# Attention and PReLU layer on one core: units 8 to 17 in five two-unit visits instead of nine groups, with a new order of chunks 1 to 3

## The chip, the core and the metric

The kernel runs on one core of a Trainium2 chip. The metric is the device time of one execution in microseconds. Five engines work side by side and wait for each other through semaphores: TensorE (PE in the profile, its weight loads PEld), VectorE (DVE), ScalarE (ACT), GpSimd (POOL) and SyncE (SP), which here only issues transfers. Each engine works through its own instructions in the order of the program.

## The reference

Linear attention with a decay per head, in blocks of positions with a running state, and behind it a two-layer network with a PReLU. Inputs are q, k and v of (4 batches, 8 heads, 768 positions, 64), a decay per head, and the weights.

```python
intra = np.einsum('bhic,bhjc->bhij', qb, kb) * Dmask[None]
intra = np.einsum('bhij,bhjd->bhid', intra, vb)
inter = np.einsum('bhid,bhde->bhie', qb * lam_pow[None], kv_state)
out[:, :, sl] = intra + inter
kv_state = lam_block[None, :, None, None] * kv_state + np.einsum('bhsd,bhse->bhde', kb * rev_pow[None], vb)
...
h = x @ w_in                                             # x: (3072, 512), w_in: (512, 2048)
g = np.maximum(h, 0.0) + alpha * np.minimum(h, 0.0)
return g @ w_out                                         # w_out: (2048, 512)
```

## The kernel before

**Units and chunks.** A unit is one batch, four heads and 256 positions; there are 24. Four units (two batches, both halves of the heads) make a chunk of 512 rows of x; there are six chunks, 0 to 5, and units 4c to 4c+3 belong to chunk c. Chunks 0 and 1 hold the first 256 positions of the batches, 2 and 3 the next, 4 and 5 the last, so unit n+8 needs the state that unit n leaves. The kernel's blocks are 128 positions long, two to a unit.

**What a unit takes.** `load(c, bi, x)` brings k, q or v of two units by a transfer from SP. `cast` makes fp16 copies on ScalarE, VectorE or GpSimd (its last argument A, V or G); `key_decayed` makes k times its decay (kdec, L284). `transposes` turns q and k over (qkT): with "D" by a DMA from SP (L302), else on TensorE with a copy. `decayed` makes q times its decay, qdT (L350), and from chunk 2 on also qdX (L362, two on GpSimd), the same rows for the other half of the partitions. The state R of a unit is kept in fp16; RX is a copy of it with the partition halves exchanged (L491, L625, GpSimd).

**Groups on TensorE.** The attention matmuls use quarters of the array (64x64). `cluster(old, new)` (L372) takes one earlier unit and one new one: the old unit's output from the state (L398), the new one's scores (L415), the old one's output from masked scores (L427), and the new one's state product (L442); then VectorE masks the scores (sm, L453) and updates R (L478), and the output is copied to xT. `visit(olds, news, engs)` (L541) takes up to two of each with one set of switches: per old unit 8 + 16 output matmuls (L509, L521), per new one 16 scores (L593) and 32 state matmuls for two (L573). The first new unit's scores lie in banks s0 and s1, the second's in tk and op, and the first old unit's outputs in two banks h. The masks (L603) follow each scores group on VectorE; the state is updated later, by `settle(n)` (L615, L625). Before, units 16 to 23 go by visits, 8 to 15 by clusters.

**The network.** `up(c, f)` is four full matmuls of 128x512 (L746) into a bank, `m = relu(-h)` on ScalarE (L756) and, at once or later by `slope_product`, `g = (1 - alpha) m + h` on VectorE (L778). A bank is free again when its slope is done; h has two, the others (op, tk, s0, s1) one each. `down(c, t, part, 4)` is four matmuls over f = 4 part to 4 part + 3 (L793); four parts make one output tile, which ScalarE copies (L806) and SP stores, at once or by `store_held`.

**The order** is written out by hand: one list of calls, L833 to the end, is the program, and each engine takes its own instructions in the order of the list. Ups and downs of the chunk before lie between the attention groups. Tiles have a few buffers each (qkT, qdT and qdX three, fp16 casts and kdec four, masks two for each half, acc one), so a call also waits for the last reader of the buffer that it takes. An instruction that waits holds up everything behind it on its engine, on SP too.

Of the kernel before, what the change touches and what calls it, by code (L numbers as in the profile page):

```python
# [11 lines left out]
def kernel(  # L12
# [24 lines left out]
    B, H, S, D = q.shape  # L37
# [503 lines left out]
    def visit(olds, news, engs, banks=("tk", "op")):  # L541
# [191 lines left out]
    G = {}  # L733
# [232 lines left out]
    up(0, 5, None, "op", True)  # L966
    slope_product(0, 5, None)
    load(1, 1, "v", None)
    gate(1, "out")
    transposed(4, 1, "A", "tk")  # L970
    up(0, 13, None, "h")
    transposes(5, "A", False)
    decayed(5, "G")
    cast(7, "k16", "G")
    load_wout(2)
    cluster(None, 4)
    up(0, 15, None, "h")
    up(0, 9, None, "op", True)
    slope_product(0, 9, None)
    up(0, 12, None, "h", True)  # L980
    cast(6, "k16", "A")
    load_wout(3)
    slope_product(0, 12, None)
    gate(3, "in")
    key_decayed(6, "G")
    cluster(4, 5, "A")
    cast(6, "q16", "A")
    down(0, 0, 0, 4, "h")
    down(0, 2, 0, 4, "op")
    transposes(6, "A", False)  # L990
    load(2, 0, "k", None)
    cast(7, "q16", "G")
    cluster(5, None, "A")
    down(0, 3, 0, 4, "h")
    decayed(6, "G")
    transposes(7, "V", False)
    up(1, 6, 0, "s1")
    up(1, 5, 0, "s0")
    down(0, 1, 0, 4, "tk")
    down(0, 2, 1, 4, "op")  # L1000
    cast(6, "v16", "V")
    decayed(7, "G")
    cast(8, "k16", "G")
    key_decayed(7, "V")
    down(0, 3, 1, 4, "h")
    cluster(None, 6)
    cast(7, "v16", "A")
    load(2, 1, "q", None)
    cast(11, "q16", "G")
    down(0, 2, 2, 4, "op")  # L1010
    down(0, 0, 1, 4, "h")
    load(2, 0, "q", None)
    cast(9, "k16", "G")
    cast(8, "q16", "G")
    cluster(6, 7, "A")
    load(2, 1, "k", None)
    key_decayed(10, "G")
    down(0, 0, 2, 4, "h")
    query_decay(2, 0)
    down(0, 2, 3, 4, "op")  # L1020
    down(0, 1, 1, 4, "tk")
    down(0, 1, 2, 4, "tk")
    cluster(7, None, "A")
    key_decayed(8, "V")
    down(0, 1, 3, 4, "tk", True)
    load(2, 0, "v", None)
    cast(8, "v16", "G")
    key_decayed(9, "G")
    up(1, 6, 1, "op")
    transposes(8, "D", False)  # L1030
    load(3, 0, "k", None)
    down(0, 0, 3, 4, "h", True)
    down(0, 3, 2, 4, "h")
    store_held(0, 0)
    query_decay(1, 0)
    cast(10, "k16", "A")
    decayed(8, "G")
    cast(9, "q16", "A")
    up(1, 5, 1, "tk", True)
    transposes(9, "D", False)  # L1040
    cast(11, "k16", "G")
    slope_product(1, 5, 1)
    up(1, 7, None, "op", True)
    slope_product(1, 7, None)
    up(1, 13, None, "h")
    cast(10, "q16", "G")
    down(0, 3, 3, 4, "h")
    cluster(None, 8)
    store_held(0, 1)
    decayed(9, "G")  # L1050
    cast(9, "v16", "A")
    up(1, 10, None, "tk")
    up(1, 1, None, "h", True)
    slope_product(1, 1, None)
    up(1, 4, None, "op")
    up(1, 11, None, "h")
    load(2, 1, "v", None)
    transposes(10, "D", False)
    up(1, 9, None, "tk")
    cluster(8, 9, "A")  # L1060
    up(1, 0, None, "op", True)
    slope_product(1, 0, None)
    decayed(10, "G")
    up(1, 8, None, "h")
    up(1, 2, None, "h")
    cast(10, "v16", "A")
    cast(11, "v16", "G")
    up(1, 3, None, "tk")
    up(1, 15, None, "op", True)
    slope_product(1, 15, None)  # L1070
    up(1, 12, None, "h")
    transposes(11, "D", False)
    decayed(11, "G")
    key_decayed(12, "V")
    load(3, 0, "q", None)
    cast(13, "q16", "A")
    load(3, 1, "q", None)
    load(3, 0, "v", None)
    cluster(9, 10, "V")
    up(1, 14, None, "tk")  # L1080
    key_decayed(13, "V")
    down(1, 2, 0, 4, "h")
    cast(12, "v16", "A")
    down(1, 0, 0, 4, "h")
    down(1, 0, 1, 4, "h")
    down(1, 2, 1, 4, "h")
    down(1, 0, 2, 4, "h")
    down(1, 2, 2, 4, "h")
    cast(12, "k16", "V")
    load(3, 1, "k", None)  # L1090
    cast(14, "q16", "A")
    cast(14, "k16", "A")
    load(4, 0, "k", None)
    down(1, 1, 0, 4, "op")
    cast(12, "q16", "G")
    cast(13, "k16", "A")
# [230 lines left out]
```

## Time and profile before

| | us |
|---|---|
| median of three runs (211.29 to 212.5) | 212.08 |
| the profiled execution: its own time | 212.1 |
| its span, first to last instruction | 210.3 |
| TensorE busy | 203.0 |
| VectorE busy | 130.9 |
| ScalarE busy | 118.9 |
| GpSimd busy | 98.1 |

The granted TensorE clock is 0.999. The page gives an engine's busy time as a share of the span. The chain of waits follows the work that ended last back to its start; in its rows stand start, length and piece, and what it calls PE is time in which nothing but TensorE's own matmuls set the end. A view of an engine in order of time gives start, length, line, operation, output and input, and in brackets the idle time before it with what ended it. In views that group instructions stand mean or min/median/max in ns.

### The profile page before, as it was taken

The page shows a single profiled execution, that of the slowest core. Times are in us where ns is not written, and L with a number is a line of the kernel's source. Part 1 is how long each engine was busy: PE and PEld are TensorE (multiplying, and loading weights), DVE is VectorE, ACT ScalarE, POOL GpSimd, SP SyncE. Part 2 cuts the span into 40 slices and gives each one's busy share as a digit, 9 for nine tenths or more (in the row PEclk, how much of TensorE's full clock was granted, in tenths as well). Part 3 has the DMA queues.
Part 4 walks back from the last instruction along what each step waited for, and adds up shares of the span by engine and source line. Part 5 has one row for each costly group of instructions (what it writes and reads, how often), then busy time and mean ns, then how long its engine had stood idle before and what let it go on. Part 6 is the DMA issues. An engine that isn't in the chain of part 4 may idle for free.

```text
span 210.3 us, 5338 instructions
## 1 busy us (share of the span) xinstructions
PE 203.0 (97%) x2145; PEld 103.4 (49%) x2145; DVE 130.9 (62%) x254; ACT 118.9 (57%) x231; POOL 98.1 (47%) x155
## 2 busy tenths in 40 slices
PE   7896999999999999999999999999999999999994
PEld 7463445645545545455454544544544444444442
DVE  7894689575299959779968774654754444444000
ACT  4995679734777454567757546565533643444121
POOL 7286088415498846589806728529464000000000
PEclk9999999999999999999999999999999999999999
DMA  5999999999999999799539999123101101110212
GB/s 156 299 280 204 227 270 269 210 261 274 222 301 167 304 218 260 174 251 221 113 107 211 232 226 228 51 51 100 51 4 53 50 2 50 53 50 0 100 50 103
DMA packets 62335, 33.91 MB, mean 161 GB/s; under 512 B 18134, under 2 KB 59366, under 8 KB 62310
## 3 DMA queue, kind: packets, MB, share of 16 engines
q1 hardware_dynamic: 58038, 29.37, 55.9%
q0 software_dynamic: 4224, 4.19, 12.1%
q8 instruction: 17, 0.28, 0.6%
q14 instruction: 8, 0.07, 0.1%
q10 hardware_dynamic: 48, 0.01, 0.0%
HBM read 27.27 MB, written 6.29 MB: 160 GB/s over the span
## 4 chain that ended last, share of the span: by engine, by line
PE 90%; DMA 3%; ACT 2%; SPq 1%; issue 1%; DVE 1%; POOL 0%; ACTq 0%
PE h_ps L746 40%; PE o_ps L793 32%; PE o_ps L822 7%; DMA vraw<-in_v_dram 3%; SPq L93 1%; PE s L415 1%; PE acc L427 1%; PE unread L147 1%; PE tp L312 1%; PE s L593 1%; PE acc L398 1%; PE acc L442 1%; PE acc L675 1%; PE acc L521 1%; ACT xT L254 1%
## 5 line engine op out<-in xcount | busy, mean ns | idle before, releaser
L778 DVE SCALAR_TENSOR_TENSOR g<-m,oma,h_ps 128x512 f16<-128x512 f32 (+1 forms) x98 | 70.8, 735 | 46.1 <-ACT m L756 43.6
L746 PE MATMUL h_ps<-xT,w_in_sb 128*128 128x512 f16 (+1 forms) x392 | 92.4, 375 | 0.1
L756 ACT ACTIVATE m<-h_ps 128x512 f32<-128x512 f32 (+1 forms) x98 | 57.5, 587 | 44.2 <-PE h_ps L746 42.4
L793 PE MATMUL o_ps<-w_out_sb,g 128*128 128x512 f16 x320 | 78.3, 379 | 0.0
L746 PEld LDWEIGHTS <-w_in_sb 128*128 128x128 f16 x392 | 37.2, 98 | 42.4 <-issue 0.6
L793 PEld LDWEIGHTS <-g 128*128 128x128 f16 x320 | 30.7, 98 | 36.2 <-issue 0.2
L350 POOL TENSOR_TENSOR qdT<-qkT,qdecay 128x512 f16<-128x512 f16 (+1 forms) x22 | 22.1, 1007 | 15.4 <-ACT qkT L254 10.5
L806 ACT ACTIVATE o_sb<-o_ps 128x512 f32<-128x512 f32 (+2 forms) x25 | 14.5, 580 | 22.4 <-PE o_ps L793 11.4
L362 POOL TENSOR_TENSOR qdX<-qkT,qdecay 64x256 f16<-64x256 f16 x32 | 22.4, 701 | 2.3
L453 DVE TENSOR_TENSOR sm<-s,dmask 128x512 f16<-128x512 f32 x24 | 15.4, 683 | 4.5 <-PE s L415 4.5
L284 POOL TENSOR_TENSOR kdec<-kraw,kdecay 128x512 f16<-128x512 f32 x14 | 14.6, 1047 | 3.4 <-DMA kraw<-in_k_dram 3.1
L254 ACT ACTIVATE xT<-acc 128x512 f16<-128x512 f32 x18 | 10.7, 596 | 8.7 <-PE acc L442 4.0
L625 POOL COPY RX<-R 64x128 f16<-64x128 f16 x16 | 5.0, 310 | 21.4 <-DVE R L615 20.7
L822 PE MATMUL o_ps<-w_out_sb,g 128*128 128x512 f16 (+2 forms) x80 | 14.0, 336 | 0.0
L603 DVE TENSOR_TENSOR sm<-s,dmask 128x512 f16<-128x512 f32 x16 | 9.9, 684 | 5.0 <-PE s L593 5.0
L822 PEld LDWEIGHTS <-g 128*128 128x128 f16 x80 | 7.2, 98 | 6.9
L258 POOL CAST qk<-qraw 128x512 f16<-128x512 f32 x13 | 8.0, 618 | 2.3 <-DMA qraw<-in_q_dram 2.0
L478 DVE SCALAR_TENSOR_TENSOR R<-R,rdecay,acc 128x64 f16<-128x64 f16 x40 | 8.6, 273 | 0.4 <-ACT R L475 0.4
L254 ACT ACTIVATE v<-vraw 128x512 f16<-128x512 f32 x12 | 7.5, 624 | 2.5 <-POOL RX L491 2.5
L258 POOL CAST qk<-kraw 128x512 f16<-128x512 f32 x9 | 6.0, 662 | 6.1 <-DMA kraw<-in_k_dram 6.0
L491 POOL COPY RX<-R 64x128 f16<-64x128 f16 x16 | 6.0, 373 | 5.5 <-DVE R L478 4.8
L258 POOL CAST v<-vraw 128x512 f16<-128x512 f32 x10 | 6.2, 628 | 4.8 <-DMA vraw<-in_v_dram 4.5
(96 smaller groups left out, 165.8 us busy)
## 6 DMA issues: line engine op xcount, KB each, us to landing
out_dram<-o_sb SPq DMA_DIRECT2D x23, 256.0 KB, 3.0
qraw<-in_q_dram SPq DMA_DIRECT2D x10, 512.0 KB, 7.5
kraw<-in_k_dram SPq DMA_DIRECT2D x10, 512.0 KB, 8.1
vraw<-in_v_dram SPq DMA_DIRECT2D x10, 512.0 KB, 5.6
w_in_sb<-in_moe_w_in_dram POOLq DMA_DIRECT2D x4, 512.0 KB, 9.6
w_out_sb<-in_moe_w_out_dram POOLq DMA_DIRECT2D x4, 512.0 KB, 8.4
kraw<-in_k_dram SPq DMA_DIRECT2D x4, 256.0 KB, 4.2
qraw<-in_q_dram SPq DMA_DIRECT2D x4, 256.0 KB, 4.7
```

Of the source, the lines that this page charges most:

```text
L254: nc.scalar.activation(out, in_, AF.Copy)
L258: nc.gpsimd.tensor_copy(out=out, in_=in_)
L284: engine(eng).tensor_tensor(out=kdec, in0=kr, in1=kdecay[:, ds(4 * hh, 4), :].rearrange("p h e -> p e h").unsqueeze(3).to_broadcast([128, ...
L350: engine(eng).tensor_tensor(out=qdT[:, :, :, p], in0=t["qkT"][:, 0, :, :, p], in1=qdecay[:, hh, :, :, p], op=ALU.mult,)
L362: nc.gpsimd.tensor_tensor(out=qdX[block], in0=t["qkT"][other, 0, :, :, block], in1=qdecay[other, hh, :, :, block], op=ALU.mult,)
L453: nc.vector.tensor_tensor(out=sm, in0=s[hl], in1=mask_of(hl, hh), op=ALU.mult)
L746: nc.tensor.matmul(h_ps[:, 0:n] if bi is None else h_ps[:, 0:n].rearrange("p (e j) -> p e j", e=2), lhsT=w_in_sb[:, gi, ts(f, 128)], rhs=x ...
L756: nc.scalar.activation(m[:, 0:n], h_ps[:, 0:n], AF.Relu, scale=-1.0)
L778: nc.vector.scalar_tensor_tensor(out=g, in0=mv, scalar=oma[:, f : f + 1], in1=hv, op0=ALU.mult, op1=ALU.add)
L793: nc.tensor.matmul(o_ps, lhsT=lhs(c, f, t), rhs=w_out_sb[:, f, :], start=(f == 0), stop=(f == NF - 1),)
L806: nc.scalar.activation(o_sb[:, 0:n], o_ps[:, 0:n], AF.Copy)
L822: nc.tensor.matmul(o_ps[:, 0:n], lhsT=lhs(c, f, t), rhs=w_out_sb[:, f, ds(x, n)], start=(f == 0), stop=(f == NF - 1),)
```

## The change

The list of calls is rewritten from chunk 0's end to chunk 3, and `visit` now also takes two new units with no old one. The diff, cut to its core (the list is told below):

```diff
@@ visit
         if olds:
             outs_to_xt(olds[-1], view, engs[len(olds) - 1])
+        elif news:
+            wide_scores(news[0], ("s0", "s1"))
         for n in news[1:]:
             wide_scores(n, banks)
@@ the list of calls, five of its lines
-    cluster(None, 8)
-    cluster(8, 9, "A")
...
-    visit([15], [16, 17], "A")
+    visit([], [8, 9], "")
...
+    visit([14, 15], [16, 17], "AA")
```

- Nine groups, cluster(None, 8), (8, 9), (9, 10) and so on to (14, 15), and visit([15], [16, 17]), become five visits: ([], [8, 9]), ([8, 9], [10, 11]), ([10, 11], [12, 13]), ([12, 13], [14, 15]) and ([14, 15], [16, 17]). The states of units 8 to 17 are now updated by `settle`.
- up(0, 15) stands before the opening cluster of unit 4, not between it and cluster(4, 5). After cluster(None, 6) come three downs instead of two.
- Ups 10, 1, 4, 11, 9 and 0 of chunk 1 stand before the first visit, ups 8, 3, 2, 15, 14 and 12 and four downs between the first and the second, eight downs before the third, seven ups and four downs before the fourth, nine ups and four downs before the fifth.
- Many casts and key products change engine: the key product of unit 10 goes from GpSimd to VectorE, and stands behind the slope of up(1, 13).
- The transposes of 8 and 9, of 12 and 13, and of 15 and 14 follow each other on SP. Some stores are held longer.

Three places of the order follow. First, VectorE around the opening cluster of unit 4, before; the g rows are slopes of chunk 0, here 14, 5 and 13, then masks and state of unit 4, then slopes 15, 9 and 12, then masks and state of unit 5:

```order
L778 SCALAR_TENSOR_TENSOR g_777<-m,oma,h_ps 128x512
L778 SCALAR_TENSOR_TENSOR g_792<-m,oma,h_ps 128x512
L778 SCALAR_TENSOR_TENSOR g_809<-m,oma,h_ps 128x512
L453 TENSOR_TENSOR sm_862<-s_828,dmask 128x512
L453 TENSOR_TENSOR sm_864<-s_829,dmask 128x512
L478 SCALAR_TENSOR_TENSOR R_0_2_116<-R_0_1_115,rdecay,acc 128x64 x2
L778 SCALAR_TENSOR_TENSOR g_878<-m,oma,h_ps 128x512
L778 SCALAR_TENSOR_TENSOR g_887<-m,oma,h_ps 128x512
L778 SCALAR_TENSOR_TENSOR g_899<-m,oma,h_ps 128x512
L453 TENSOR_TENSOR sm_957<-s_907,dmask 128x512
L453 TENSOR_TENSOR sm_959<-s_908,dmask 128x512
L478 SCALAR_TENSOR_TENSOR R_1_2_121<-R_1_1_120,rdecay,acc 128x64 x2
```

The same place after; the slopes are 14, 15, 5 and 13, then unit 4, slope 9, and unit 5:

```order
L780 SCALAR_TENSOR_TENSOR g_777<-m,oma,h_ps 128x512
L780 SCALAR_TENSOR_TENSOR g_799<-m,oma,h_ps 128x512
L780 SCALAR_TENSOR_TENSOR g_801<-m,oma,h_ps 128x512
L780 SCALAR_TENSOR_TENSOR g_827<-m,oma,h_ps 128x512
L453 TENSOR_TENSOR sm_882<-s_848,dmask 128x512
L453 TENSOR_TENSOR sm_884<-s_849,dmask 128x512
L478 SCALAR_TENSOR_TENSOR R_0_2_116<-R_0_1_115,rdecay,acc 128x64 x2
L780 SCALAR_TENSOR_TENSOR g_905<-m,oma,h_ps 128x512
L453 TENSOR_TENSOR sm_962<-s_912,dmask 128x512
L453 TENSOR_TENSOR sm_964<-s_913,dmask 128x512
L478 SCALAR_TENSOR_TENSOR R_1_2_121<-R_1_1_120,rdecay,acc 128x64 x2
```

Slope 15 has moved ahead of slope 5 and of the masks and the state of unit 4, and slope 12 behind unit 5; between the two groups one slope is left of three.

Second, VectorE where unit 8 is opened, before; the slopes are 7 and 13 of chunk 1, then masks and state of unit 8, slopes 10, 1, 4, 11 and 9, and the mask of unit 9:

```order
L778 SCALAR_TENSOR_TENSOR g_1307<-m,oma,h_ps 128x512
L778 SCALAR_TENSOR_TENSOR g_1316<-m,oma,h_ps 128x512
L453 TENSOR_TENSOR sm_1361<-s_1327,dmask 128x512
L453 TENSOR_TENSOR sm_1363<-s_1328,dmask 128x512
L478 SCALAR_TENSOR_TENSOR R_0_3_97<-R_0_2_96,rdecay,acc 128x64 x2
L478 SCALAR_TENSOR_TENSOR R_0_4_98<-R_0_3_97,rdecay,acc 128x64 x2
L778 SCALAR_TENSOR_TENSOR g_1386<-m,oma,h_ps 128x512
L778 SCALAR_TENSOR_TENSOR g_1395<-m,oma,h_ps 128x512
L778 SCALAR_TENSOR_TENSOR g_1404<-m,oma,h_ps 128x512
L778 SCALAR_TENSOR_TENSOR g_1413<-m,oma,h_ps 128x512
L778 SCALAR_TENSOR_TENSOR g_1425<-m,oma,h_ps 128x512
L453 TENSOR_TENSOR sm_1486<-s_1436,dmask 128x512
```

After; the slopes are 11 and 9, then the masks of units 8 and 9 by the visit, slope 0, the state of unit 8, and slopes 8, 3 and 2:

```order
L780 SCALAR_TENSOR_TENSOR g_1372<-m,oma,h_ps 128x512
L780 SCALAR_TENSOR_TENSOR g_1381<-m,oma,h_ps 128x512
L605 TENSOR_TENSOR sm_1441<-s,dmask 128x512
L605 TENSOR_TENSOR sm_1443<-s,dmask 128x512
L605 TENSOR_TENSOR sm_1463<-s,dmask 128x512
L605 TENSOR_TENSOR sm_1465<-s,dmask 128x512
L780 SCALAR_TENSOR_TENSOR g_1467<-m,oma,h_ps 128x512
L617 SCALAR_TENSOR_TENSOR R_0_3_97<-R_0_2_96,rdecay,acc 128x64 x2
L617 SCALAR_TENSOR_TENSOR R_0_4_98<-R_0_3_97,rdecay,acc 128x64 x2
L780 SCALAR_TENSOR_TENSOR g_1482<-m,oma,h_ps 128x512
L780 SCALAR_TENSOR_TENSOR g_1494<-m,oma,h_ps 128x512
L780 SCALAR_TENSOR_TENSOR g_1503<-m,oma,h_ps 128x512
```

Four masks now stand together, with the slopes of 8, 3 and 2 behind them and the state of unit 8; the state of unit 9 comes later still.

Third, SP from the loads of chunk 2 on, before; the loads are k of units 8 and 9, q of both pairs, k of 10 and 11, and behind the store v of 8 and 9, and the transposes are those of 8, 9, 10 and 11:

```order
L93 DMA kraw<-in_k_dram 128x8x128
L93 DMA qraw<-in_q_dram 128x8x128 x2
L93 DMA kraw<-in_k_dram 128x8x128
L815 DMA out_dram<-o_sb 128x512
L93 DMA vraw<-in_v_dram 128x8x128
L302 DMA_TRANSPOSE qkT<-qk_1064 128x8x128
L93 DMA kraw<-in_k_dram 128x8x128
L815 DMA out_dram<-o_sb 128x512
L302 DMA_TRANSPOSE qkT<-qk_1133 128x8x128
L815 DMA out_dram<-o_sb 128x512 x2
L93 DMA vraw<-in_v_dram 128x8x128
L302 DMA_TRANSPOSE qkT<-qk_1281 128x8x128
```

After; the loads are q of both pairs, k of 8 and 9, and behind the store v of 8 and 9, k of 12 and 13, k of 10 and 11, the transposes are those of 8, 9 and 10, and the 1x1 transfer is a gate, which only waits for a part of the weights:

```order
L93 DMA qraw<-in_q_dram 128x8x128 x2
L119 DMA gates_153<-w_in_sb 1x1
L93 DMA kraw<-in_k_dram 128x8x128
L817 DMA out_dram<-o_sb 128x512
L93 DMA vraw<-in_v_dram 128x8x128
L93 DMA kraw<-in_k_dram 128x8x128 x2
L302 DMA_TRANSPOSE qkT<-qk_1209 128x8x128
L302 DMA_TRANSPOSE qkT<-qk_1231 128x8x128
L817 DMA out_dram<-o_sb 128x512 x2
L93 DMA vraw<-in_v_dram 128x8x128
L93 DMA kraw<-in_k_dram 128x8x128
L302 DMA_TRANSPOSE qkT<-qk_1318 128x8x128
```

The load of k of units 10 and 11 has moved from ahead of the first store to behind v of 8 and 9 and k of 12 and 13; the transposes of 8 and 9 stand behind it, side by side.

More of the change, by code (lines that the diff above doesn't have):

```diff
@@ L1005 @@
[L1005 to L1012, printed above, removed]
+    cluster(7, None, "A")
     cast(9, "k16", "G")
     cast(8, "q16", "G")
[L1015 to L1021, printed above, removed]
+    cast(11, "q16", "G")
+    key_decayed(9, "G")
@@ L1072 @@
+    load(3, 0, "q", None)
+    store_held(0, 0)
     transposes(11, "D", False)
[L1073 to L1076, printed above, removed]
     load(3, 1, "q", None)
     load(3, 0, "v", None)
[L1079 to L1088, printed above, removed]
```

332 lines of the change are left out of this document (177 added, 155 removed).

## The prediction

> **What bounds the kernel now.** I read the page's busy shares first, then its slices, then stretches of time engine by engine, then the chain of work that ended last. The page:
>
> ```profile
> PE 203.0 (97%) x2145; PEld 103.4 (49%) x2145; DVE 130.9 (62%) x254; ACT 118.9 (57%) x231; POOL 98.1 (47%) x155
> DMA  5999999999999999799539999123101101110212
> ```
>
> TensorE is busy for 203.0 of 210.3 us, and the DMA engines are at nine tenths or more in nearly all of the first half, where the change lies. Stretches show where TensorE still waits, and what is near it (after the colon: stretch, then busy time of PE, PEld, DVE, ACT, POOL).
>
> ```profile
> 30.00:40.00 10.00, 9.84 (x151) 5.51 (x148) 8.92 (x17) 8.84 (x20) 7.68 (x11) 1.00 1.19 245
> 40.00:120.00 80.00, 80.00 (x1028) 40.61 (x1021) 61.00 (x122) 48.65 (x93) 50.50 (x75) 1.00 0.97 220
> 60.00:70.00 10.00, 10.00 (x142) 4.99 (x143) 9.76 (x21) 7.43 (x13) 8.76 (x15) 1.00 1.05 233
> ```
>
> From 40 to 120 us TensorE has no gap; from 30 to 40 it lacks 0.16 us. So the only things that can move the time are matmul time itself and new gaps. And VectorE, at 9.76 of 10, has nothing to spare just where the first new visit comes. The chain gives TensorE's own cost of a cluster and a visit (start, length, piece):
>
> ```profile
> 57.60 0.86 PE o_ps L793 x4
> 58.47 0.35 PE s L415 x16
> 58.94 4.42 PE h_ps L746 x20
> 63.36 0.24 PE acc L398 x8
> ...
> 64.17 5.29 PE h_ps L746 x24
> ...
> 71.23 6.91 PE o_ps L793 x32
> ...
> 106.88 0.24 PE acc L509 x8
> ...
> 108.03 2.78 PE h_ps L746 x12
> ...
> 118.58 0.24 PE ot L509 x8
> ...
> 120.07 0.97 PE h_ps L746 x4
> ```
>
> Four full matmuls take 6.91 / 8 = 0.863 us. A cluster with an old and a new unit runs from 63.36 to 64.17, and the 24 matmuls behind it take 5.29 where 6 x 0.863 = 5.18 would do: 0.81 + 0.11 = 0.92 us. The opening cluster (new unit only) takes 58.94 - 58.47 = 0.47 and 0.10 behind it, 0.57. The visit of one old and two new units: 108.03 - 106.88 = 1.15, and 2.78 - 2.59 = 0.19 behind it, 1.34. A full visit (two and two): 120.07 - 118.58 = 1.49, and 0.97 - 0.863 = 0.11 behind it, 1.60, against 1.84 for two clusters.
>
> **Term 1, fewer groups: -0.93 us.** Before, units 8 to 17 cost 0.57 + 7 x 0.92 + 1.34 = 8.35 us of TensorE. After, four full visits are 6.40. The opening visit has no row: it is the opening cluster with a second unit's 32 quadrant matmuls. At least it costs 0.57 (they run beside the first), at most 2 x 0.57 = 1.14; a full visit less its two output parts lies nearer to the upper end, so I take 1.02. Sum 7.42, a gain of 0.93, between 0.8 and 1.4. All of it is on the path. The matmul counts are otherwise equal.
>
> **Term 2, chunk 0's end: +0.4 us.** up(0, 15) moves from behind the opening cluster of unit 4 to a place before it. So two ups instead of three now stand between that cluster and cluster(4, 5), whose first matmuls wait for the state of unit 4. VectorE, ScalarE and TensorE before:
>
> ```profile
> 33.11 0.75 DVE L778 SCALAR_TENSOR_TENSOR g<-m,oma,h_ps 128x512 f16<-128x512 f32 x1 [0.20 <-ACT m L756]
> 33.77 1.28 DVE L453 TENSOR_TENSOR sm<-s,dmask 128x512 f16<-128x512 f32 x2
> 35.03 0.47 DVE L478 SCALAR_TENSOR_TENSOR R<-R,rdecay,acc 128x64 f16<-128x64 f16 x2
> ```
>
> ```profile
> 32.48 0.60 ACT L756 ACTIVATE m<-h_ps 128x512 f32<-128x512 f32 x1
> 33.23 1.02 ACT L254 ACTIVATE qkT<-tp 128x1024 f16<-128x1024 f16 x1 [0.16 <-PE tp L312]
> ```
>
> ```profile
> 32.53 0.61 PE L312 MATMUL tp<-ident,qk 128*128 128x128 f16 x8
> ...
> 36.14 0.28 PE L387 MATMUL acc<-qdT,RD 128*128 128x128 f16 x2
> ```
>
> From the transposes at 32.53 to the state's end at 35.50 are 2.97 us, and TensorE comes for it at 36.14, 3.61 us after the transposes: 0.64 us of cover. One up less leaves 2.75, so the cover is gone by 0.22. Besides, VectorE's order is now slope 15, slope 5, slope 13, masks, state. The transposes start at 33.45 (0.863 later, and behind one more m of ScalarE, 0.06). The m of up 15 ends at 32.87 (TensorE's 32.07, 0.2 to start, 0.60). Three slopes of 0.69, two masks in 1.28 and the state in 0.47 end at 36.7, against TensorE's 33.45 + 2.75 = 36.2: 0.5 us of wait. Before, TensorE waited here a little later for the q cast of unit 6 (a part of the 0.16 us above); that wait is absorbed, so I take 0.4, between 0.1 (only the 0.22 counts, less the absorbed part) and 0.6.
>
> **Term 3, VectorE at the opening visit: +0.65 us.** The before program opens unit 8 at 58.47; the after program does the same work and six more ups first (10, 1, 4, 11, 9, 0), so it gets there at 58.47 + 5.18 + 0.4 = 64.05. The rows that price VectorE here:
>
> ```profile
> 58.94 1.28 DVE L453 TENSOR_TENSOR sm<-s,dmask 128x512 f16<-128x512 f32 x2
> 60.13 0.85 DVE L478 SCALAR_TENSOR_TENSOR R<-R,rdecay,acc 128x64 f16<-128x64 f16 x4
> ...
> 66.66 4.21 DVE L778 SCALAR_TENSOR_TENSOR g<-m,oma,h_ps 128x512 f16<-128x512 f32 x6
> ```
>
> Two masks 1.28 (1.19 to the next start), four states 0.77, a slope 0.69 back to back. Masks started 0.47 us after their scores in the chain's terms (58.47, 58.94). In the visit 32 state matmuls go ahead of the scores, about 0.35 us, so the masks of unit 8 run from 64.87 to 66.15. TensorE leaves the visit at 65.07, does up(1, 8) in bank h until 65.93, and then wants bank s1 for up(1, 3), which the second mask has still to read: 0.2 us, 0.3 with the semaphore. Then VectorE has the masks of unit 9 (to 67.35), slope 0 (68.05), four states (68.8) and slopes 8, 3, 2 (70.9). TensorE has done its six ups at 65.07 + 0.3 + 5.18 = 70.55, and down(1, 0) needs g of 0 to 3: 0.35 us more. Before, one cluster put two masks before VectorE; here it is four at once, and no slope may pass them. Least 0.2 us, if the masks start when the scores do; most 1.0, if ScalarE's m is late too. Between these ends I stay at 0.65, since the row that is nearest is the same mask on the same engine.
>
> In that stretch key_decayed(10) is now on VectorE, ahead of slopes 1, 4, 11 and 9:
>
> ```profile
> L284 DVE TENSOR_TENSOR kdec<-kraw,kdecay x10: 678/744/1072, 6.4 to 113.9; 128x512 f16<-128x512 f32 x10
> 50.47 1.07 POOL L258 CAST qk<-kraw 128x512 f16<-128x512 f32 x1
> ```
>
> The median of 0.744 us is in the sum: slope 13 ends near 60.8, and 0.74 and four slopes end at 64.3, just in time. The Trainium skill, page "SBUF — State Buffer", section "SBUF: two separate sides", says that VectorE instructions with two SBUF inputs and GpSimd instructions take a shared port as an exclusive lock, the later one standing still; by this rule, which speaks against the change since both engines wait for the same load of k here, the product would take its slowest 1.07 us and the sum would be 0.3 us higher. The trace bears the rule out once, a GpSimd cast of 1.07 us.
>
> **At nothing.** Casts and key products that change engine or place, held stores and the later loads cost nothing while TensorE runs on: six ups, 5.2 us, hide the casts of units 10 to 12, eight downs, 6.9 us, hide those of 12 and 13, and the last two visits have 9.5 and 11.2 us of matmuls ahead of them. Without cover each cast costs its own 0.4 to 0.6 us. The SP queue is the exception, in the second rival.
>
> **Sum.** The profiled execution's own time is 212.1 (span 210.3, and 1.8 around it), equal to the median of the runs, 212.08. 212.1 - 0.93 + 0.4 + 0.65 = **212.2 us**; with the terms' ends 211.0 (212.1 - 1.4 + 0.1 + 0.2) to 212.9 (212.1 - 0.8 + 0.6 + 1.0).
>
> **Rivals.** *The waits don't show.* If VectorE's order costs nothing, 212.1 - 0.93 = 211.2, with the gain's upper end 210.7. For it: before, every such wait is covered from 40 us on. Against it: 9.76 of 10 us busy on VectorE.
>
> *A load that comes late: slower.* On SP k of units 10 and 11 stood before v of units 8 and 9; now it stands behind that and behind k of units 12 and 13. GpSimd waits for it with four casts and products, and only then makes both decayed queries of units 8 and 9, two key products, RX of unit 8, the decayed query of unit 10, and RX of unit 9, for which the second visit waits.
>
> ```profile
> 51.20 0.99 SPq L93 DMA_DIRECT2D vraw<-in_v_dram  x1
> ```
>
> ```profile
> 58.34 1.16 POOL L350 TENSOR_TENSOR qdT<-qkT,qdecay 128x512 f16<-128x512 f16 x1
> ...
> 61.05 0.61 POOL L258 CAST qk<-kraw 128x512 f16<-128x512 f32 x1
> ...
> 62.27 0.64 POOL L491 COPY RX<-R 64x128 f16<-64x128 f16 x2
> L284 POOL TENSOR_TENSOR kdec<-kraw,kdecay x14: 1037/1047/1059, 15.8 to 148.3; 128x512 f16<-128x512 f32 x14
> ```
>
> ```profile
> out_dram<-o_sb SPq DMA_DIRECT2D x23, 256.0 KB, 3.0
> DMA to landing us min/median/max: 3.3/4.4/5.9
> DMA to landing us min/median/max: 3.1/5.9/8.5
> ```
>
> The last two rows are the transposes between 50 and 120 us, and all loads of k. With v issued at 51.4, k of 10 and 11 is issued near 52.5 and lands at 58.4 by the median, 61.0 by the slowest. The transpose of unit 9 waits for a cast behind the m of up(1, 10), near 58.7, and lands at 63.1 (62.0 to 64.6). Behind both GpSimd needs 3 x 2.71 + 2 x 1.05 + 2 x 0.7 = 11.6 us: RX at 74.7. TensorE comes for it at 74.0 + 0.65 + 0.5 = 75.1 (four downs after 70.9, and the first outputs and scores). So 0.4 us of cover: with the median landings nothing is lost; with the slowest transpose 1.1, and beyond a k landing of 61 us each us late is a us lost, and the transposes of units 12 and 13, queued on SP behind the same wait, come as late for the third visit. Slowest case of the transposes at both visits: 212.2 + 1.1 + 0.9 = 214.2. The Trainium skill, page "Advanced Engine Details and Errata", section "X-Bar Transpose (TRN2)", says that transposes are as fast as other DMAs; by it unit 9's would land like a store of the same 256 KB, 3.0 us, and this rival would need a late k alone. The trace has 4.4 against 3.0.
>
> *The change does not do what it says*: the order shows the transposes of 8 and 9, 12 and 13, and 14 and 15 side by side, but not those of 10 and 11. No price of its own.
>
> **How the numbers follow.** Forecast (waits eat the gain): 0.45. Waits don't show, 210.7 to 211.5: 0.2, half of it over 0.5% below 212.1. Late load: 0.35, mostly above 213.1. 0.5%, 1.06 us, is about what a measurement of this kernel can tell from no change. Faster 0.1, within 0.55 (0.45 and the other half of 0.2), slower 0.35. The forecast alone spans 211.0 to 212.9; with the rivals, leaving out a tenth on each side, 211.0 to 214.4.
>
> **What would show it.** Term 1: the costs of groups 8 to 17 on TensorE sum to 7.4 us. Term 2: a gap of some 0.4 us before the first output matmuls of cluster(4, 5), ended by VectorE's R. Term 3: gaps of 0.3 us before up(1, 3) and before down(1, 0), ended by a mask and a slope. Late load: GpSimd idle on kraw past 61 us, and a gap inside the second or third visit ended by RX, by decayed queries or by a transpose. I am wrong if TensorE has no gap at these places, or if a gap of over 1 us stands at another.

## The result, and the profile after

The changed kernel takes 213.96 us (median of 7 runs, 213.41 to 214.28) against 212.2 us for the kernel before on the same chip (7 runs): ratio 1.0077, 95% interval 1.0053 to 1.0101. It is slower, by 1.6 us of the 212. The prediction's range (211.0 to 214.4) holds the time; its likeliest case (212.2) did not come, its second rival (a late load) named the two visits where most of the loss lies, and its slowest case (214.2) comes near the time, though not for the reason given and in size partly by luck. The profiled execution took 213.82 us, its span 211.7.

The page's first rows, and the stretches (after the colon: stretch, then busy time of PE, PEld, DVE, ACT, POOL):

```profile
PE 204.2 (96%) x2145; PEld 104.0 (49%) x2145; DVE 132.3 (62%) x257; ACT 115.8 (55%) x230; POOL 100.0 (47%) x158
```

```profile
30.00:40.00 10.00, 9.54 (x142) 5.27 (x144) 8.49 (x18) 8.56 (x19) 7.82 (x10) 1.00 1.14 239
40.00:120.00 80.00, 78.92 (x941) 39.81 (x942) 61.57 (x124) 45.05 (x89) 51.06 (x76) 1.00 0.91 205
60.00:70.00 10.00, 9.81 (x106) 4.64 (x105) 9.79 (x18) 6.59 (x13) 9.45 (x13) 1.00 1.05 201
70.00:80.00 10.00, 9.89 (x150) 5.02 (x148) 8.15 (x22) 5.39 (x12) 6.86 (x13) 1.00 1.03 257
80.00:90.00 10.00, 9.22 (x146) 4.72 (x145) 7.84 (x16) 5.25 (x10) 8.92 (x13) 1.00 0.73 169
```

Before, TensorE had no gap from 40 to 120 us; now it lacks 1.08 us there, 0.78 of it between 80 and 90, and 0.46 instead of 0.16 between 30 and 40. TensorE's own rows name the places (start, length, line, what; in brackets the idle time ahead and what ended it):

```profile
36.54 0.27 PE L387 MATMUL acc<-qdT,RD 128*128 128x128 f16 x2 [0.37 <-DVE R L478]
...
65.80 4.48 PE L748 MATMUL h_ps<-xT,w_in_sb 128*128 128x512 f16 x20 [0.19 <-DVE sm L605]
70.11 3.62 PE L795 MATMUL o_ps<-w_out_sb,g 128*128 128x512 f16 x16
73.66 0.24 PE L509 MATMUL ot<-qdT,R 64*64 64x128 f16 x1
...
74.39 0.59 PE L509 MATMUL acc<-qdX,RX 64*64 64x128 f16 x2
...
75.68 7.08 PE L795 MATMUL o_ps<-w_out_sb,g 128*128 128x512 f16 x32
82.69 0.24 PE L509 MATMUL ot<-qdT,R 64*64 64x128 f16 x1
...
83.73 0.21 PE L509 MATMUL acc<-qdX,RX 64*64 64x128 f16 x1 [0.25 <-POOL qdX L362]
84.48 0.21 PE L509 MATMUL acc<-qdX,RX 64*64 64x128 f16 x1 [0.53 <-POOL qdX L362]
...
85.41 4.59 PE L748 MATMUL h_ps<-xT,w_in_sb 128*128 128x512 f16 x20
```

Four places: before cluster(4, 5); behind the opening visit; inside the visit of old 8 and 9; inside that of old 10 and 11. A matmul's end is modelled and overlaps the next, so idle time in brackets is too small: the true loss is read from start to start. The second visit lasts from 73.66 to 75.68, 2.02 us, the third from 82.69 to 85.41, 2.72, where the fourth takes 1.52: waits of about 0.5 and 1.2 us. Both end on GpSimd, as its rows show:

```profile
59.74 1.18 POOL L258 CAST qk<-kraw 128x512 f16<-128x512 f32 x2 [1.17 <-DMA kraw<-in_k_dram]
60.88 1.49 POOL L284 TENSOR_TENSOR kdec<-kraw,kdecay 128x512 f16<-128x512 f32 x1
...
72.40 1.59 POOL L362 TENSOR_TENSOR qdX<-qkT,qdecay 64x256 f16<-64x256 f16 x2
74.05 0.99 POOL L627 COPY RX<-R 64x128 f16<-64x128 f16 x3
77.52 0.29 POOL L627 COPY RX<-R 64x128 f16<-64x128 f16 x1 [2.48 <-DVE R L617]
77.89 1.05 POOL L284 TENSOR_TENSOR kdec<-kraw,kdecay 128x512 f16<-128x512 f32 x1
79.00 0.64 POOL L627 COPY RX<-R 64x128 f16<-64x128 f16 x2
79.70 0.61 POOL L258 CAST v<-vraw 128x512 f16<-128x512 f32 x1
80.61 3.82 POOL L362 TENSOR_TENSOR qdX<-qkT,qdecay 64x256 f16<-64x256 f16 x4 [0.30 <-DMA qkT<-qk]
```

From 59.74, when k of 10 and 11 has landed, GpSimd works through to 74.70, when RX of unit 9 is done (the two copies from 74.05). TensorE came for it at 74.3. Then GpSimd stands 2.48 us, since RX of unit 10 waits for a state that VectorE makes behind four masks; behind it come the key product of unit 14, RX of 11, a cast of v of 13, two qdX of unit 12 and only then two of unit 11, for which TensorE waits.

To compare traces, I take one stretch with the same network matmuls in all kernels: from the first up behind the first four half transposes (25.15 before, 25.02 after) to the first full matmul behind the last of the five visits (107.96 before, 109.45 after): **82.81 us before, 84.43 after, +1.62**. It leaves out the first 25 us, which vary by 1.8 us from one profiled execution of these kernels to the next, ahead of everything that the edits touch. Its parts, from start to start and with the 0.1 us that TensorE loses ahead of each group: the nine groups took 8.2 us, the five visits would take 7.4 without waits, **-0.84**; before cluster(4, 5) 0.53 lost and 0.17 saved at the transposes behind it, **+0.36**; behind the opening visit **+0.36** (4.48 us row at 65.80, 1.23 us after the up at 64.57 instead of 0.86); second visit **+0.48**; third **+1.22**. Sum +1.58.

### The profile page after: what moved, and what is told of

Read it like the earlier page. It is cut to its first block, busy times and chain, and to the rows that moved or that the text cites. A ratio compares the mean times of both kernels' runs of the same rounds, so it can differ in the third digit from the quotient of the medians.

```text
span 211.7 us, 5336 instructions
## 1 busy us (share of the span) xinstructions
PE 204.2 (96%) x2145; PEld 104.0 (49%) x2145; DVE 132.3 (62%) x257; ACT 115.8 (55%) x230; POOL 100.0 (47%) x158
## 4 chain that ended last, share of the span: by engine, by line
PE 86%; POOL 3%; SPq 3%; DMA 2%; DVE 2%; issue 2%; ACT 1%; DVEq 0%; ACTq 0%; POOLq 0%
PE h_ps L748 38%; PE o_ps L795 31%; PE o_ps L824 7%; SPq L93 3%; DMA vraw<-in_v_dram 2%; PE s L595 2%; POOL qdX L362 2%; PE unread L147 1%; PE tp L312 1%; PE acc L573 1%; PE acc L521 1%; PE ot L509 1%; PE s L415 1%; PE ot L521 1%; DVE sm L453 1%
## 5 line engine op out<-in xcount | busy, mean ns | idle before, releaser
L795 PEld LDWEIGHTS <-g 128*128 128x128 f16 x320 | 30.8, 98 | 36.4 <-DVE g L780 0.2
L350 POOL TENSOR_TENSOR qdT<-qkT,qdecay 128x512 f16<-128x512 f16 (+1 forms) x20 | 19.8, 991 | 11.4 <-ACT qkT L254 7.0
L362 POOL TENSOR_TENSOR qdX<-qkT,qdecay 64x256 f16<-64x256 f16 x32 | 23.6, 736 | 2.5 <-DMA qkT<-qk 0.3
L284 POOL TENSOR_TENSOR kdec<-kraw,kdecay 128x512 f16<-128x512 f32 x17 | 18.5, 1098 | 2.1 <-DMA kraw<-in_k_dram 1.8
L627 POOL COPY RX<-R 64x128 f16<-64x128 f16 x32 | 9.3, 291 | 17.1 <-DVE R L617 15.6
L254 ACT ACTIVATE xT<-acc 128x512 f16<-128x512 f32 x16 | 9.5, 597 | 7.5 <-PE acc L442 2.5
L258 POOL CAST qk<-kraw 128x512 f16<-128x512 f32 x12 | 7.8, 662 | 10.2 <-DMA kraw<-in_k_dram 10.1
L617 DVE SCALAR_TENSOR_TENSOR R<-R,rdecay,acc 128x64 f16<-128x64 f16 x48 | 10.2, 273 | 0.0
L258 POOL CAST qk<-qraw 128x512 f16<-128x512 f32 x10 | 6.1, 613 | 2.8 <-DMA qraw<-in_q_dram 2.8
L147 PE MATMUL unread<-ident 128*128 128x512 f16 x23 | 6.6, 413 | 0.3 <-DVE qkT L256 0.3
L595 PE MATMUL s<-qkT 64*64 64x128 f16 x256 | 6.6, 218 | 0.0
```

The lines of the kernel that those rows point to most:

```text
L258: nc.gpsimd.tensor_copy(out=out, in_=in_)
L284: engine(eng).tensor_tensor(out=kdec, in0=kr, in1=kdecay[:, ds(4 * hh, 4), :].rearrange("p h e -> p e h").unsqueeze(3).to_broadcast([128, ...
L350: engine(eng).tensor_tensor(out=qdT[:, :, :, p], in0=t["qkT"][:, 0, :, :, p], in1=qdecay[:, hh, :, :, p], op=ALU.mult,)
L362: nc.gpsimd.tensor_tensor(out=qdX[block], in0=t["qkT"][other, 0, :, :, block], in1=qdecay[other, hh, :, :, block], op=ALU.mult,)
L595: nc.tensor.matmul(s[hl][ds(a * 64, 64), hp, 1 - e, :].rearrange("p (e j) -> p e j", e=2), lhsT=t["qkT"][p, 1, e, hp, ds(a * 64, 64)], rhs ...
L795: nc.tensor.matmul(o_ps, lhsT=lhs(c, f, t), rhs=w_out_sb[:, f, :], start=(f == 0), stop=(f == NF - 1),)
```

## The experiments

Theory: the two waits in the second and third visit make the kernel slower, and they stand in series: GpSimd and the loads set when they end, so that what is won or lost ahead of the last one is swallowed by it. First rival: each gap is paid by itself, so that the gaps add up. Second rival, on the cause of the third visit's wait: GpSimd has too much to do, or a transpose lands late, and the order on GpSimd matters little. All runs are in one table; waits are not subtracted from the visits, which take 1.5 us without any. The last column counts from the start of the execution, so it is to be read with the column before it: an execution that begins the stretch earlier brings TensorE earlier to every place behind.

| kernel | ratio to before, interval | stretch us | second visit | third visit | stretch begins | end of third |
|---|---|---|---|---|---|---|
| the change | 1.0077 (1.0053 to 1.0101) | 84.43 | 2.02 | 2.72 | 25.02 | 85.41 |
| r1_bank | 1.0108 (1.0065 to 1.0151) | 84.34 | 2.42 | 2.37 | 25.13 | 85.43 |
| r2_visit3 | 1.0043 (1.0015 to 1.0072) | 84.12 | 2.90 | 1.50 | 24.57 | 84.63 |
| r3_visit2 | 1.0089 (1.0056 to 1.0122) | 85.45 | 1.54 | 3.32 | 23.84 | 85.25 |
| r4_both | 1.0038 (1.0014 to 1.0062) | 83.18 | 1.54 | 1.50 | 24.19 | 83.32 |
| r5_three | 1.0009 (0.9989 to 1.0029) | 82.64 | 1.54 | 1.50 | 24.85 | 83.44 |
| r6_four | 1.0003 (0.9972 to 1.0034) | 82.30 | 1.54 | 1.50 | 24.88 | 83.13 |
| r7_loads | 1.0232 (1.0196 to 1.0268) | 88.05 | 2.30 | 5.09 | 23.42 | 86.46 |
| r8_kdec | 1.0081 (1.0052 to 1.0110) | 83.97 | 2.42 | 1.50 | 24.28 | 84.20 |
| r9_kfirst | 1.0077 (1.0048 to 1.0105) | 83.97 | 1.82 | 2.39 | 24.59 | 84.52 |
| r10_fill | 1.0090 (1.0058 to 1.0121) | 84.77 | 1.54 and the fill | 2.68 | 24.36 | 85.09 |
| r11_fill5 | 1.0016 (0.9991 to 1.0042) | 83.51 | 1.54 and the fill | 1.50 | 25.21 | 84.67 |
| r12_five | 0.9972 (0.9946 to 0.9998) | 82.33 | 1.56 | 1.50 | 23.91 | 82.19 |

**Banks exchanged (r1_bank).**

```diff
-    up(1, 3, None, "s1")
-    up(1, 2, None, "s0")
+    up(1, 3, None, "s0")
+    up(1, 2, None, "s1")
```

> The changed kernel with the banks of up(1, 3) and up(1, 2) exchanged, so that the first of the two takes the bank whose mask is done first. Both theories expect the gap of 0.37 us behind up(1, 8) at 65.4 us to go. Theory in series: the two later waits for GpSimd (0.53 us in the second visit, 1.23 us in the third) end at times that GpSimd sets, so TensorE only arrives earlier and waits longer there: the waits in the second and third visit together grow by 0.3 to 0.4 us and the time stays at 213.96 (within 0.2). Rival, each gap paid by itself: 213.96 - 0.37 = 213.6, with the later waits as they were.

The row that waited is gone; ups and downs now follow each other:

```profile
64.68 5.53 PE L748 MATMUL h_ps<-xT,w_in_sb 128*128 128x512 f16 x24
70.05 3.66 PE L795 MATMUL o_ps<-w_out_sb,g 128*128 128x512 f16 x16
```

But from 64.68 to 70.05 are 5.37 us for 24 matmuls that need 5.18: 0.19 come back inside the row, so only some 0.15 us were freed. The third visit ends at 85.43 as before the edit. That fits the series, but the freed time is too small to tell the two apart, and the interval of the ratio holds both forecasts.

**Unit 11 ahead of unit 12 (r2_visit3).**

```diff
     cast(13, "v16", "G")
+    decayed(11, "V")
     decayed(12, "V")
...
     cast(12, "v16", "V")
-    decayed(11, "V")
```

> The changed kernel with the decayed queries of unit 11 made ahead of those of unit 12, behind the second visit. Theory: the third visit waits for the qdX of unit 11, which stands on GpSimd behind the qdX of unit 12, which the fourth visit needs and which waits for a transpose that lands at 80.6 us. With the order exchanged the qdX of unit 11 ends near 81.7, before TensorE comes at 83.3; the 1.23 us go: 213.96 - 1.2 = 212.7. Rival: GpSimd has simply more to do than fits between the two visits, and the order of two equal pieces changes only what TensorE waits for there: the transposes of 12 or 13 then hold the scores or the fourth visit waits, and the time falls by less than 0.4 us, 213.6 or more.

The third visit takes 1.50 us: its wait is gone, and neither the scores nor the fourth visit (1.53 us) wait instead. The ratio falls from 1.0077 to 1.0043, 0.7 us, with intervals that overlap, and the new one holds both forecasts (212.7 and 213.6 are 1.0024 and 1.0066 of 212.2). The stretch falls only by 0.3, because in this execution the second visit, which lies ahead of the edit, waits longer, now for the state of unit 9 on VectorE:

```profile
73.58 0.39 PE L595 MATMUL s<-qkT 64*64 64x128 f16 x16
74.73 0.21 PE L509 MATMUL acc<-qdT,R 64*64 64x128 f16 x1 [0.75 <-DVE R L617]
```

```profile
71.79 1.31 DVE L256 CAST qk<-kraw 128x512 f16<-128x512 f32 x1
73.02 0.89 DVE L256 CAST qk<-qraw 128x512 f16<-128x512 f32 x1
73.83 0.84 DVE L617 SCALAR_TENSOR_TENSOR R<-R,rdecay,acc 128x64 f16<-128x64 f16 x4
```

Two casts for unit 12, which the second visit does not need, stand ahead of that state. So exchanging the order is enough to take the third wait away, with GpSimd's work the same. The edit moves VectorE's part of the decayed query of unit 11 too, but in the change that part was done at 83.16, before TensorE came for it at 83.27, so the wait was GpSimd's. That the order alone made the wait does not follow: r8_kdec, below, removes it by taking work out.

**State of unit 9 earlier (r3_visit2), and both (r4_both).**

```diff
     key_decayed(13, "G")
+    settle(9)
     load(3, 1, "k", None)
...
     cast(12, "q16", "V")
-    settle(9)
```

> The changed kernel with the state of unit 9 (VectorE) and its copy RX (GpSimd) moved ahead of the decayed query of unit 10, to behind the slopes of up(1, 8), up(1, 3) and up(1, 2). Both theories expect the wait of 0.53 us inside the second visit, ended by RX of unit 9, to go. Theory in series: TensorE comes 0.5 us earlier to the third visit, whose qdX of unit 11 hangs on a transpose that lands near 80.6 us, so the wait there grows from 1.23 to about 1.7 us and the time stays at 213.96 (within 0.25). Rival, each gap paid by itself: 213.96 - 0.53 = 213.4.

> Both moves together: the state of unit 9 earlier, and the decayed queries of unit 11 ahead of those of unit 12. Theory: with the third visit's wait gone nothing swallows the 0.53 us any more: 213.96 - 1.23 - 0.53 = 212.2, the time of the kernel before. Rival (GpSimd has more to do than fits): the waits come back at the third or fourth visit and the time stays above 212.9.

With the state alone the second visit waits no more (1.54), and the third waits longer (3.32 instead of 2.72):

```profile
83.05 0.21 PE L509 MATMUL acc<-qdT,R 64*64 64x128 f16 x1 [0.36 <-DVE qdT L350]
83.58 0.21 PE L509 MATMUL acc<-qdX,RX 64*64 64x128 f16 x1 [0.32 <-POOL qdX L362]
84.32 0.21 PE L509 MATMUL acc<-qdX,RX 64*64 64x128 f16 x1 [0.53 <-POOL qdX L362]
```

The time is not lower (1.0089), but that does not decide for the series: the edit made a new wait of 0.44 us at the downs, where the state of unit 9 now stands ahead of the last three slopes of VectorE, and 0.48 less 0.44 leaves nothing to swallow. What the trace does show is that TensorE, which began the stretch 1.2 us earlier in this execution (23.84), came to the third visit 0.76 us earlier than in the change (81.93, 82.69) and left it only 0.16 earlier (85.25, 85.41): the transpose of unit 12, for which the qdX wait, landed at 80.3 us here and at 80.5 in the change. With both moves both visits are clean, the stretch is 83.18 and the ratio 1.0038. The same new wait is there, 0.45 us, and the pieces add up: -0.48 - 1.22 + 0.45 = -1.25, which is what the stretch lost of the expected 1.76. The interval leaves out the expected 1.000; the time fits the rival's (above 212.9), but no wait came back in the third or fourth visit.

```profile
69.29 2.75 PE L795 MATMUL o_ps<-w_out_sb,g 128*128 128x512 f16 x12
72.31 1.04 PE L795 MATMUL o_ps<-w_out_sb,g 128*128 128x512 f16 x4 [0.27 <-DVE g L780]
```

**Three and four moves (r5_three, r6_four).** The state of unit 9 now goes behind the slope of up(1, 12), the banks are exchanged, and in the second kernel up(0, 15) goes back:

```diff
     up(1, 12, None, "h")
+    settle(9)
+    decayed(10, "G")
...
     cluster(None, 4)
+    up(0, 15, None, "h")
```

> The changed kernel with three moves: decayed queries of 11 ahead of those of 12; the state of unit 9 and its RX ahead of the decayed query of unit 10 and now behind the slope of up(1, 12), so that no slope waits for them; and the banks of up(1, 3) and up(1, 2) exchanged. Theory (the last wait swallows those before it, and with it gone each counts): the 1.23, 0.53 and 0.37 us go, some 0.15 us may come back at the first downs, where the slope of up(1, 2) ends late: 2.0 us below the changed kernel, that is 0.998 to 1.000 of the kernel before. Rival (GpSimd has more to do than fits, a wait returns later): 1.003 or more of the kernel before, and a wait of over 0.5 us ended by GpSimd in the third or fourth visit.

> The three moves and a fourth: up(0, 15) back behind the opening cluster of unit 4. Theory: the gap of 0.37 us before cluster(4, 5) goes, as before the change, and since nothing late is left behind it the time falls by 0.3 to 0.4 us below the three moves: 0.996 to 0.998 of the kernel before, the gain of fewer groups (0.9 us) less what small waits are left. Rival: the loads and GpSimd go by their own clock and take the 0.37 us back at the second or third visit: the same time as with three moves.

Three moves: stretch 82.64, no row of TensorE waits in the visits, ratio 1.0009, just above the expected 1.000. Four moves: the matmuls of cluster(4, 5) follow the ups without a gap, and the stretch falls by 0.34 to 82.30:

```profile
33.27 2.76 PE L748 MATMUL h_ps<-xT,w_in_sb 128*128 128x512 f16 x12
35.87 0.28 PE L387 MATMUL acc<-qdT,RD 128*128 128x128 f16 x2
```

So this gap is paid in full here; whether the later waits of the changed kernel would have swallowed it, no run tests. The ratios 1.0009 and 1.0003 are too close to tell the two kernels apart by time. The ratio of 1.0003 lies above the expected 0.996 to 0.998, which its interval reaches; the stretch is 0.51 us below that of the kernel before, not 0.9: 0.2 us is left at up(1, 12), 0.1 behind the third visit.

**Why the third visit waits (r7_loads, r8_kdec).**

```diff
-    load(3, 1, "q", None)
-    load(3, 0, "v", None)
...
     transposes(12, "D", False)
+    load(3, 1, "q", None)
+    load(3, 0, "v", None)
```

> The changed kernel with the loads of q of units 14 and 15 and of v of 12 and 13 moved from ahead of the transpose of unit 12 to behind it on SP, nothing else. It tells why the third visit waits. If the late transpose alone is the cause, the transpose lands some 3 us earlier (near 77.5 instead of 80.6 us), the four qdX of GpSimd start earlier and the wait of 1.23 us falls by 0.9 or more: 213.0. If GpSimd's own work ahead of them (RX of 10 from 77.5 us, the key product of 14, RX of 11, the cast of v of 13, until 80.3 us) binds as closely as the transpose, the four qdX can start only 0.3 us earlier and the wait falls by 0.3, or not at all if v of 13 then comes late: 213.6 to 214.0.

Neither branch held: it is the slowest kernel of all, 1.0232, with a third visit of 5.09 us. The transpose is issued earlier, but v of 12 and 13 is now late, and GpSimd's cast of it holds everything behind:

```profile
80.77 0.79 POOL L258 CAST v<-vraw 128x512 f16<-128x512 f32 x1 [2.11 <-DMA vraw<-in_v_dram]
81.64 3.20 POOL L362 TENSOR_TENSOR qdX<-qkT,qdecay 64x256 f16<-64x256 f16 x4
```

So this run says nothing on the transpose. Nor is all of its loss that wait: the 44 full matmuls between the third and the fourth visit take 10.66 us instead of 9.70. The granted clock, the number behind POOL's count, fell to 0.50 there, after TensorE had been busy for only 0.66 of the 3 us from 82 to 85; the six runs of this kernel have mean granted clocks of 0.984 to 0.992.

```profile
82.00:84.00 2.00, 0.34 (x12) 0.10 (x2) 1.40 (x3) 0.69 (x3) 1.87 (x3) 1.00 0.91 154
84.00:86.00 2.00, 1.32 (x61) 1.09 (x64) 0.00 (x0) 0.06 (x1) 0.77 (x2) 0.81 0.95 250
86.00:88.00 2.00, 2.00 (x20) 0.88 (x21) 1.29 (x2) 1.06 (x2) 1.86 (x3) 0.50 0.93 248
88.00:90.00 2.00, 2.00 (x9) 0.87 (x8) 0.75 (x1) 1.14 (x2) 1.30 (x3) 0.84 0.88 166
```

The next run takes the key product of unit 14 out of GpSimd's list ahead of the third visit:

```diff
     settle(10)
-    key_decayed(14, "G")
     settle(11)
...
+    key_decayed(14, "G")
     decayed(13, "G")
```

> The changed kernel with the key product of unit 14 (GpSimd, 1.05 us, needed by the fourth visit only) moved from between the second and third visit to behind the third. If GpSimd's work alone makes the third visit wait, the wait falls by 1.05 us: 212.9. If the transpose of unit 12, landing at 80.6 us, binds just as closely, the qdX of unit 12 still starts at 80.6 and the wait stays within 0.2 us of what it was: 213.8 to 214.0. If the late transpose and the work bind together, neither this run nor the one with the loads moved wins more than 0.4 us, though the exchange of two pieces on GpSimd took the whole wait away.

In the profiled execution the third visit's wait is gone (1.50): the four qdX start at 79.38 instead of 80.61. The transpose of unit 12 landed 5.7 us after its issue there, at 79.2, while it took 7.0 and landed at 80.5 in the trace of the change. The times do not show it: 213.23 us against 211.68 before, 1.0081, the ratio of the change itself; the profiled execution (212.82) is the third fastest of nine. Its stretch is only 0.46 us shorter than that of the change, because the second visit waits 0.40 us longer, and so small a fall lies within the interval. The other traces with this order and this work tell what binds. In r1_bank, r9_kfirst and r10_fill the four qdX start without a wait, at 81.14, 79.89 and 81.23 us, the transpose having landed at 79.7, 79.2 and 77.2, and the third visit still waits 0.9 to 1.2 us; in the change and in r3_visit2 they wait 0.30 and 0.39 us for the transpose. So GpSimd's list alone is enough for the wait, and a late transpose adds to it in some executions; how often it does in those without a trace stays open.

**Load of k first (r9_kfirst).**

```diff
     load(2, 0, "v", None)
+    load(2, 1, "k", None)
     load(3, 0, "k", None)
```

> The changed kernel with the load of k of units 10 and 11 issued ahead of the load of k of 12 and 13 on SP, nothing else. The prediction's rival named this late load as the head of GpSimd's chain to RX of unit 9. If it is, GpSimd starts its casts 0.7 us or more before 59.7 us and RX of unit 9 ends as much before 74.7: the wait of 0.53 us in the second visit goes, and the third visit's wait, which stands on its own, grows by as much (time unchanged, 1.006 to 1.009 of the kernel before). If the transpose of unit 10 (landing at 71.0 us) and the state of unit 9, behind a cast that waits for the load of q of 12, bind as closely, RX of unit 9 still ends within 0.3 us of 74.7 and the second visit keeps a wait of 0.3 us or more; the time is unchanged too.

```profile
58.07 1.17 POOL L258 CAST qk<-kraw 128x512 f16<-128x512 f32 x2 [1.12 <-DMA kraw<-in_k_dram]
...
62.10 1.16 POOL L350 TENSOR_TENSOR qdT<-qkT,qdecay 128x512 f16<-128x512 f16 x1 [0.83 <-DMA qkT<-qk]
...
73.81 0.64 POOL L627 COPY RX<-R 64x128 f16<-64x128 f16 x2 [0.29 <-DVE R L617]
```

The second branch, by a hair: GpSimd starts 1.67 us earlier and gives it back, 0.83 to the transpose of unit 9 and 0.29 to the state of unit 9; RX ends at 74.45 instead of 74.70. The second visit still waits 0.28 us (1.82), and the time is the same, 1.0077. The load of k was one of three equal heads, not the head. The third visit's wait did not grow as expected, but is 0.33 us less than in the change; the transpose of unit 12 landed 1.3 us earlier here.

**Added matmuls (r10_fill, r11_fill5).**

```diff
+    fill(4, "s0")
     visit([8, 9], [10, 11], "AA")
```

> The changed kernel with four more full matmuls (0.86 us, a result that nothing reads) on TensorE directly ahead of the second visit: added work that the reference does not ask for. Theory in series: TensorE waits there anyway for GpSimd and the transposes (0.53 us in the second visit, 1.23 us in the third), so the added 0.86 us come out of these waits and the time stays within 0.3 us of the changed kernel, 1.006 to 1.010 of the kernel before. Rival, each gap paid by itself: 0.86 us more, 1.0118.

> The same four added matmuls at the same place in the kernel with three moves, in which no wait follows: both theories expect the full 0.86 us, less at most 0.2: 1.004 to 1.005 of the kernel before, against 1.001 without them. If the time does not rise here either, the added matmuls cost less than they look and the run above says nothing.

In the change 0.86 us of added matmuls leave the ratio at 1.0090 (1.0077 without). That lies in the theory's range, but the rival's 1.0118 lies inside the interval too, so the times do not decide. The trace does not bear out the theory in series. The second visit loses its wait (1.54 instead of 2.02): 0.48 of the 0.86 us are swallowed by the wait directly behind them, which the rival's sum leaves out. But the third visit still waits 1.18 us (1.22 in the change), and the stretch grows by 0.34 us, about what is left. The third visit ends at 85.09, before the change's 85.41, but this execution began the stretch 0.66 us earlier. GpSimd's rows say why:

```profile
77.59 0.29 POOL L627 COPY RX<-R 64x128 f16<-64x128 f16 x1 [3.21 <-DVE R L617]
...
81.23 2.88 POOL L362 TENSOR_TENSOR qdX<-qkT,qdecay 64x256 f16<-64x256 f16 x4
```

GpSimd's list for the third visit begins with RX of unit 10, whose state comes behind masks of the second visit's scores, and VectorE waited 1.09 us for those scores here. A second visit that comes later so starts the list for the third one later; it does not run on a clock of its own. In the kernel with three moves the added matmuls lengthen the stretch by 0.87 us (83.51 against 82.64); its times show less, 212.32 against 212.03 us, with intervals of 0.2 to 0.25% that allow for it.

So the series is not shown. In these traces the gaps add up, except that a wait swallows what is put directly ahead of it, up to its own length, and that a late transpose can hold TensorE at a fixed time (r3_visit2).

**Best version (r12_five).** The four moves, and:

```diff
-    settle(8)
     up(1, 8, None, "h")
+    settle(8)
```

> The kernel with four moves, and the state of unit 8 one slope later (behind that of up(1, 8)): in its trace up(1, 12) waits 0.16 us for that slope. Theory: the 0.16 us go and nothing else moves; with the 0.9 us of fewer groups this is 0.7 us below the kernel before: 0.995 to 0.998 of it. Rival: the loads and GpSimd set the second half of this stretch, and a wait returns in the second to fifth visit: 1.000 or more.

211.26 us against 211.84 before, 0.9972 (0.9946 to 0.9998), within the expected range, and the lowest median of all, though the interval overlaps that of four moves. The range was not met by the step named, and so in part by luck: the ups now run without loss (63.17 to 68.36, 5.19 us), while the downs behind them lose 0.2 us, and the stretch is that of four moves, 82.33.

```profile
63.17 5.35 PE L748 MATMUL h_ps<-xT,w_in_sb 128*128 128x512 f16 x24
68.36 3.83 PE L795 MATMUL o_ps<-w_out_sb,g 128*128 128x512 f16 x16
```

## Why the prediction was right or wrong, step by step

- **Term 1** (-0.93) measured -0.84. The opening visit, which had no row, took 0.93 us with its switch (estimated 1.02), a full visit 1.6. Shown in the end by the kernels with four and five moves: their stretch is 0.5 us below that of before, with 0.3 us of small waits left in it.
- **Term 2** (+0.4) measured +0.36. The state was done at 36.4 (36.7 forecast) and TensorE was there at 36.0 (36.2). Shown by r6_four.
- **Term 3** (+0.65): the first half, the second mask ahead of up(1, 3), measured 0.36 (0.3 forecast). The second half, 0.35 us at down(1, 0), did not come. VectorE began the masks at 64.45, not 64.87, so slope 2 ended near 70.3, not 70.9, before the third matmul of the down that began at 70.11. VectorE had nothing to spare there all the same: 0.77 us of state put ahead of its last slopes cost 0.45 (r4_both).
- **At nothing**: this step failed. "eight downs, 6.9 us, hide those of 12 and 13" counted the casts, and not GpSimd. Behind the second visit GpSimd takes from 77.52 to 84.43 for what stands ahead of the qdX of unit 11 and for these, 6.9 us that begin only when VectorE is done with four masks and a state. That was to be seen in the order: the decayed query of 12 stands ahead of that of 11, and the third visit needs only the latter. It cost 1.2 us, the largest piece of the loss. Shown by r2_visit3 and, with less work ahead, by r8_kdec.
- **The late load** was named as a rival with a chance of 0.35, at the second visit, by RX of unit 9, and at the third. RX was done at 74.70, the forecast's 74.7 to the digit, in part by luck: the list began at 62.88 behind GpSimd's own casts, not at 63.1 with the transpose, and took 11.8 us instead of 11.6. The failing number was the other one. The 75.1 does not follow from the forecast's own figures: four downs after 70.9 are 74.35, and with 0.5 for the first outputs and scores 74.85, a cover of 0.15 us. And TensorE came at 74.3, because Term 3's second half was missing and the visit began early, so the cover turned into a wait of 0.5. The forecast's sentence "with the median landings nothing is lost" fell with it. The sign named for it, GpSimd idle on kraw past 61 us, did not come (59.74), and the load of k was not the sole head (r9_kfirst). At the third visit the forecast's 0.9 us came from the slowest transpose alone; GpSimd's list made it 1.2. So 1.1 and 0.9 us were forecast and 0.5 and 1.2 came: that the time lies near 214.2 is luck.
- **The shared port.** VectorE's key product of unit 10 took 0.99 us and GpSimd's of unit 11 beside it 1.49, where 0.74 and 1.05 are usual. This agrees with the rule of the Trainium skill, page "SBUF — State Buffer", section "SBUF: two separate sides", and each engine lost once: VectorE's product began at 60.46 beside a GpSimd cast that ran to 60.92, GpSimd's at 60.88 beside VectorE's, which ran to 61.45. VectorE's slopes were done in time for the masks all the same. **The transposes** landed 3.1 to 8.1 us after their issue between 54 and 95 us, while the three stores of the same 256 KB there took 4.7 by the median; that they are as fast as other transfers (the Trainium skill, page "Advanced Engine Details and Errata", section "X-Bar Transpose (TRN2)") holds about for their median of 5.0.

## What to carry to other kernels

Where work is regrouped for one engine, list for every group what each other engine must have done by then, in that engine's own order, and add up everything ahead of it, also what a later group needs; the largest cost of this change was two pieces of GpSimd's list in the wrong order. Before a later wait is held to swallow what is won ahead of it, look at what starts the other engine's list: here it started with the scores of the visit before, so most gaps added up. And look for the wait that an edit makes elsewhere: read each edit by all gaps in the trace, and not by the time alone. With the order mended, the regrouping is worth about 0.5 us of 212 in the traces; the times of the two best kernels (1.0003 and 0.9972) allow for it.

## What the runs showed of the hardware

- GpSimd's four qdX took 3.82 us beside VectorE's casts and decayed queries (in the change and in r8_kdec), and 2.88 us in r10_fill, where VectorE was done at 80.7, before they began; a pair alone takes 1.40. In r10_fill the pieces ahead were longer instead, beside VectorE's decayed queries and cast (RX of unit 11 1.07 and the cast of v 0.95 us, where the change has 0.64 and 0.61). Against these shorter times GpSimd's list for the third visit lost 0.94 us in the change and 0.77 in r10_fill: by this estimate most of the third visit's wait is two engines slowing each other, wherever in the list it falls.
- Either engine can lose: VectorE's cast of k of unit 12 took 0.42 us in r5_three, where GpSimd's decayed query beside it took 1.65, and 1.31 us in r2_visit3, where GpSimd's took 1.16.
- The same transpose of the same size, issued at 72.4 to 74.1 us, landed after 3.9 us (r2_visit3), 4.3 (r10_fill), 5.7 to 5.8 (six runs), 6.3 to 6.7 (three) and 7.0 (the change). A sum with one landing time for it can't be right within a microsecond.
- The granted clock stayed at 1.00 behind the second visit of r2_visit3, where TensorE had been busy for 0.27 us of the one from 74 to 75, and fell to 0.50 in r7_loads after it had been busy for 0.66 us of three.
